# Routed attention and a PReLU feed-forward: key chunks in pairs, another first feed-forward, cluster scores on column tiles

## The chip, the cores and the metric

The kernel runs on one core of a Trainium2 chip. Its time is the device time of one execution in microseconds (us), as the median of the runs of one measurement. A profile is one further execution, taken by the hardware profiler. The engines are TensorE (PE in the rows; PEld are its weight loads), VectorE (DVE), ScalarE (ACT), GpSimd (POOL) and SyncE (SP), whose queue issues most of the DMA transfers. Each engine works through its own instructions in program order.

## The reference

Attention over 4 batches, 8 heads, 768 positions and head width 64, in which a query sees only the keys whose nearest of 16 centroids is the same; then a feed-forward of 512 to 2048 to 512 with a learned negative slope.

```
q_assign = argmax(einsum(q_n, c_n)); k_assign = argmax(einsum(k_n, c_n))
mask = q_assign[..., :, None] == k_assign[..., None, :]
scores = where(mask, q @ k.T / 8, -1e9)
attn = exp(scores - max); attn = attn / (sum(attn) + 1e-9)
x = (attn @ v) as (3072, 512)
h = x @ w_in;  g = max(h, 0) + alpha * min(h, 0);  out = g @ w_out
```

The weights of the feed-forward arrive as 64-bit floats, and the kernel makes 32-bit ones of them itself.

## The kernel before

Two heads make a pair; there are 16 pairs (4 batches of 4). The queries of a batch are worked on in two halves of 384. A **unit** (`units`, L264) is one pair, one half and one chunk of 128 keys: 6 units make a pair's half, 24 a **block** (one batch, one half), 192 the kernel. So there are 8 blocks, 0 to 7, each of which ends with one tile `xT`, the input of a feed-forward of 384 rows.

`score` (L271) multiplies a chunk of keys with the half's queries for both heads (tile `sps`, L277), takes the exponential on ScalarE (`E`, L282), zeroes on VectorE what lies in another cluster (the mask, L285), and adds `E` into `acc` on VectorE (L291, L293), from which the softmax denominators come. `weigh` (L296) multiplies `E` with the values (`vps`, L317), three units behind `score` (`LAG`). At a pair's last chunk it sums `acc` over the keys with a matmul (L306), inverts the sum (`rd`, L309), notes the lowest one (`lowest`, L312), and writes `xT` (L322). The two heads use halves of TensorE: `score` contracts over 64 rows for each head, `weigh` writes 64 columns for each; the feed-forward uses all 128 by 128. An fp32 matmul of the program shows as two rows of the profile, so `x4` at L277 or L317 is one unit.

A pair is prepared ahead of its first unit by `prep_features` (12 transposes, L208, copied by ScalarE into `qkT`, L212, with squares, L216), `prep_clusters` (12 matmuls of 32 columns, L224, and four VectorE steps up to `first`, the cluster of each position) and `prep_queries` (L251, `aq`). All of them write the one PSUM buffer of `misc()`, the tile `mps`.

The feed-forward of a block runs inside the next block, in pieces (`ffn_pieces`, L326): 16 of `hidden` (L335, then two ScalarE and one VectorE step into `gT`) and 12 of `final` (L352, into the output rows `y`). The weight conversion (`convert`, L154) takes 32 pieces: a DMA of 512 KB into `raw` (two buffers), four VectorE steps with two ScalarE steps between them, and a product on GpSimd. The conversions come from unit 20 on, two to a unit from unit 26.

The loop at L382 writes all of this out in one order for every engine: `score`, then preparation, conversions, feed-forward pieces, then `weigh`. Nothing reorders it later.

## Time and profile before

| | |
|---|---|
| median of 3 runs | 1286.82 us (1284.21 to 1287.08) |
| the profiled execution | 1280.17 us |
| its span, first to last instruction | 1278.3 us |
| busy in the span: TensorE | 1152.1 us (90%) |
| VectorE | 681.9 us (53%) |
| ScalarE | 398.9 us (31%) |
| GpSimd | 46.1 us (4%) |
| mean granted TensorE clock | 0.964 |

The span is the part that the rows below describe; the execution is 1.9 us longer. Shares are means over stages with different limits, so the rows are grouped by stage: the start up to the first exponential at 34.0 us, block 0 up to 120.7, block 1 up to 321.7, blocks 2 to 6 up to 1050.0, block 7 up to the last weighting at 1182.4, and the last feed-forward.

### The profile page before, as it was taken

How to read it: one execution, taken by the hardware profiler on the slowest of the kernel's cores; microseconds unless marked ns; L12 is line 12 of the kernel's file. 1: busy time of each engine (PE TensorE's matmuls, PEld its weight loads, DVE VectorE, ACT ScalarE, POOL GpSimd, SP SyncE). 2: the span in 40 equal slices, each digit the busy share in tenths (PEclk: the TensorE clock that was granted, in tenths of full speed). 3: DMA queues.
4: the chain of work that ended last, by engine and by line, in shares of the span. 5: the costliest groups of instructions: out<-in, count | busy, mean ns of one | idle time of the engine just before them, and what ended most of it. 6: DMA issues, size and time to landing. Idle time of an engine off the chain costs nothing.

```text
span 1278.3 us, 10850 instructions
## 1 busy us (share of the span) xinstructions
PE 1152.1 (90%) x4228; PEld 527.7 (41%) x4228; DVE 681.9 (53%) x971; ACT 398.9 (31%) x718; POOL 46.1 (4%) x57
## 2 busy tenths in 40 slices
PE   4876577689899999999899999999899999999898
PEld 3431233234444335444444334444454334433553
DVE  1689999944554464544545454644544455544210
ACT  2443354422343223322343123322343123311220
POOL 0002222300000000000000000000000000000000
PEclk9997798889999999999999999999999999999899
DMA  3302334311100010011100020011100000000000
GB/s 87 95 1 69 101 116 130 115 46 46 46 1 1 17 45 1 1 46 46 46 1 1 9 54 1 1 46 46 46 0 1 9 17 1 1 9 14 3 1 26
DMA packets 62938, 42.76 MB, mean 33 GB/s; under 512 B 51600, under 2 KB 55712, under 8 KB 62880
## 3 DMA queue, kind: packets, MB, share of 16 engines
q1 hardware_dynamic: 62592, 41.95, 11.5%
q8 instruction: 35, 0.57, 0.2%
q14 instruction: 23, 0.19, 0.0%
q10 hardware_dynamic: 288, 0.04, 0.0%
HBM read 35.69 MB, written 6.29 MB: 33 GB/s over the span
## 4 chain that ended last, share of the span: by engine, by line
PE 76%; DVE 16%; ACT 4%; issue 2%; DMA 0%; SPq 0%; ACTq 0%; DVEq 0%
PE fps L352 26%; PE fps L335 24%; PE sps L277 9%; PE vps L317 9%; DVE rd L309 4%; PE mps L224 4%; DVE E L285 3%; PE mps L208 2%; DVE gT L343 2%; DVE mant L163 1%; PE mps L251 1%; DVE mant L172 1%; ACT power L166 1%; PE mps L306 1%; DVE power L161 1%
## 5 line engine op out<-in xcount | busy, mean ns | idle before, releaser
L335 PE MATMUL fps<-xT,w_in_sb 128*128 128x384 f32 x1024 | 365.9, 512 | 36.2 <-DVE xT L322 21.1
L285 DVE SCALAR_TENSOR_TENSOR E<-aq,first,E 128x384 f32<-128x384 bf16 x384 | 226.9, 632 | 301.7 <-ACT E L282 301.3
L352 PE MATMUL fps<-w_out_sb,gT 128*128 128x512 f32 x768 | 353.7, 606 | 0.0
L282 ACT ACTIVATE E<-sps 128x768 f32<-128x768 f32 x192 | 155.7, 811 | 404.5 <-PE sps L277 291.2
L335 PEld LDWEIGHTS fps<-xT,w_in_sb 128*128 128x128 f32 x1024 | 198.9, 200 | 180.6 <-issue 50.0
L352 PEld LDWEIGHTS fps<-w_out_sb,gT 128*128 128x128 f32 x768 | 140.9, 192 | 165.4 <-issue 163.9
L343 DVE SCALAR_TENSOR_TENSOR gT<-neg,alpha_neg,gT 128x384 f32<-128x384 f32 x128 | 88.2, 693 | 179.7 <-ACT neg L342 179.1
L277 PE MATMUL sps<-qkT 64*128 64x384 f32 x768 | 182.3, 552 | 1.2 <-ACT E L282 1.1
L317 PE MATMUL vps<-E,vt 128*64 128x384 f32 x768 | 168.3, 518 | 10.1 <-DVE xT L322 9.9
L341 ACT ACTIVATE gT<-fps 128x384 f32<-128x384 f32 x128 | 62.7, 490 | 236.4 <-PE fps L335 236.4
L293 DVE TENSOR_TENSOR acc<-acc,E 128x768 f32<-128x768 f32 x128 | 122.6, 958 | 4.4
L277 PEld LDWEIGHTS sps<-qkT 64*128 64x128 f32 x768 | 59.5, 190 | 118.2 <-issue 94.1
L309 DVE RECIPROCAL rd<-mps 128x384 f32<-128x384 f32 x32 | 81.7, 2553 | 23.4 <-PE mps L306 23.4
L317 PEld LDWEIGHTS vps<-E,vt 128*64 128x64 f32 x768 | 41.8, 137 | 115.7 <-issue 85.5
L208 PE MATMUL mps<-ident,qk 128*128 128x128 f32 x192 | 35.2, 312 | 32.7 <-DVE lowest L312 29.4
L342 ACT ACTIVATE neg<-fps 128x384 f32<-128x384 f32 x128 | 62.1, 485 | 0.0
L224 PEld LDWEIGHTS mps<-cT,qkT 128*128 128x128 f32 x384 | 49.0, 209 | 10.6 <-issue 7.6
L224 PE MATMUL mps<-cT,qkT 128*128 128x32 f32 x384 | 50.8, 293 | 2.2 <-ACT qkT L212 2.2
L166 ACT ACTIVATE power<-power,low_exp 128x512 uint32<-128x512 uint32 x32 | 23.1, 722 | 80.7 <-DVE power L161 80.7
L208 PEld LDWEIGHTS mps<-ident,qk 128*128 128x128 f32 x192 | 22.7, 154 | 59.8 <-issue 50.1
L357 ACT COPY y<-fps 128x512 f32<-128x512 f32 x24 | 14.1, 586 | 94.0 <-PE fps L352 94.0
L212 ACT COPY qkT<-mps 128x512 f32<-128x512 f32 x48 | 27.9, 582 | 32.4 <-PE mps L208 32.4
(54 smaller groups left out, 389.0 us busy)
## 6 DMA issues: line engine op xcount, KB each, us to landing
raw<-in_moe_w_in_dram SPq DMA_DIRECT2D x16, 512.0 KB, 3.8
raw<-in_moe_w_out_dram SPq DMA_DIRECT2D x16, 512.0 KB, 3.5
qk<-in_q_dram SPq DMA_DIRECT2D x32, 192.0 KB, 3.5
qk<-in_k_dram SPq DMA_DIRECT2D x32, 192.0 KB, 3.5
vt<-in_v_dram SPq DMA_DIRECT2D x16, 384.0 KB, 4.2
out_dram<-y SPq DMA_DIRECT2D x24, 256.0 KB, 2.1
csb<-in_centroids_dram ACTq DMA_DIRECT2D x8, 4.0 KB, 2.5
alf<-in_moe_alpha_dram ACTq DMA_DIRECT2D x1, 8.0 KB, 2.3
```

The lines of the kernel that those rows point to most:

```text
L208: nc.tensor.transpose(out=ps[:, i * P:(i + 1) * P], in_=raw_qk[n, w][:, j].rearrange("p h d -> p (h d)"), identity=ident)
L224: nc.tensor.matmul(out=ps[:, t * W:(t + 1) * W], lhsT=qkTs[n][:, t * P:(t + 1) * P], rhs=cT[:, hp * W:(hp + 1) * W], start=True, stop=True)
L277: nc.tensor.matmul(out=ps[:, h, 0:HS], lhsT=qkT[r:r + D, S + c * P:S + (c + 1) * P], rhs=qkT[r:r + D, half * HS:(half + 1) * HS], start=Tr ...
L282: nc.scalar.activation(out=E, in_=ps[:, :, 0:HS], func=AF.Exp, scale=SCALE)
L285: nc.vector.scalar_tensor_tensor(out=E[:, h, :], in0=aqs[n, half][:, h, :], scalar=first[:, t:t + 1], in1=E[:, h, :], op0=ALU.is_equal, op ...
L293: nc.vector.tensor_tensor(out=accs[n, half], in0=accs[n, half], in1=E, op=ALU.add)
L309: nc.vector.reciprocal(out=rd, in_=ps[:, 0:HS])
L317: nc.tensor.matmul(out=po[r:r + D, 0:HS], lhsT=vts[n][:, h, c, :], rhs=E[:, h, :], start=(c == 0), stop=(c == NJ - 1))
L335: nc.tensor.matmul(out=ps[:, 0:HS], lhsT=w_in_sb[:, c, f * P:(f + 1) * P], rhs=xT[:, c, :], start=(c == 0), stop=(c == NCH - 1))
L341: nc.scalar.activation(out=gs[f], in_=ps[:, 0:HS], func=AF.Relu)
L343: nc.vector.scalar_tensor_tensor(out=gs[f], in0=neg, scalar=alpha_neg[:, f:f + 1], in1=gs[f], op0=ALU.mult, op1=ALU.add)
L352: nc.tensor.matmul(out=ps[:, 0:DM], lhsT=gs[f][:, i * P:(i + 1) * P], rhs=w_out_sb[:, f, :], start=(f == 0), stop=(f == NF - 1))
```

## The change

- **Steps.** A step is now two chunks of keys (`GROUP` = 2): 96 steps, 12 to a block, 3 to a pair's half. A step runs `score` for both chunks, then `weigh` of the step before, `mask`, `normalise` of the step before, and `add_up`; feed-forward pieces (two or three to a step), preparation and conversions follow in turn.
- **Preparation** stands at whole steps: features in a pair's third step ahead, clusters in the second, queries in the last. Up to the end of block 0, `misc()` also uses the two feed-forward PSUM buffers, which nothing else needs yet. Of pair 1 nothing is prepared ahead of the first step any more.
- **Cluster scores** are 4 matmuls of 32 output rows and 384 columns, each on its own 32 columns of TensorE (`prep_sims`), a ScalarE copy, and 3 transposes, in place of 12 matmuls of 32 columns.
- **Denominators in block 0** come from TensorE matmuls over each `E` (`sum_rows`); VectorE only adds up the sums of three steps, and `acc` is left out there.
- **Conversions** start at step 1, one to a step in block 0 and two in block 1. Each call starts one conversion and finishes the one before it. The order of the pieces is by quarters of the hidden width, and the first feed-forward takes its pieces in that order, with three partial outputs to a quarter that are added into `y` (ScalarE for the first quarter, VectorE for the others).
- **At the start**, the centroids come in one transfer instead of eight, their squares are summed on VectorE, and 40 small matmuls run on TensorE.
- The `gT` step of a hidden piece is issued with the next piece.

```diff
+    for i in range(40):
+        nc.tensor.matmul(out=warm[:, 0:P], lhsT=ident_bf, rhs=ident_bf, start=True,
+                         stop=True)
...
+        def rest():
+            nc.vector.scalar_tensor_tensor(
+                out=power, in0=hi, scalar=0x80000000, in1=power,
+                op0=ALU.bitwise_and, op1=ALU.bitwise_or)
...
+    def convert_next():
+        if sources:
+            half_converted.append(convert(*sources.popleft()))
+        if half_converted and (len(half_converted) > 1 or not sources):
+            half_converted.popleft()()
+            converted[0] += 1
...
+    def prep_sims(n):
+        hp = pairs[n][1]
+        ps = misc()
+        for g in range(NG):
+            nc.tensor.matmul(out=ps[g * W:(g + 1) * W, 0:GT * P],
+                             lhsT=cT[:, hp * W:(hp + 1) * W],
+                             rhs=qkTs[n][:, g * GT * P:(g + 1) * GT * P],
+                             start=True, stop=True)
+        simTs[n] = asg.tile([P, GT * P], FP32, name="simT")
+        nc.scalar.copy(simTs[n], ps[:, 0:GT * P])
...
+        den = None
+        if u < UB:
+            den = sum_rows(E)
+        elif s == SB - 1:
+            den = sum_rows([accs.pop((n, half))])
...
-    for u in range(NU + LAG + 1):
+    for u in range(NS + 1):
...
+        if u < NS:
             score(u)
+        if u > 0:
+            weigh(u - 1)
+        if u < NS:
+            mask(u)
+        if u > 0:
+            normalise(u - 1)
+        if u < NS:
+            add_up(u)
...
+        converting = 1 if 0 < u < UB else 2 if UB <= u < 2 * UB else 0
+        for i in range(max(take, len(prep), converting)):
+            if i < take:
+                ffn.popleft()()
+            if prep:
+                prep.popleft()()
+            if i < converting:
+                convert_next()
```

The first place is TensorE's order at the start of block 2. Before, three units there read (L317 is `weigh`, L277 `score`, L335 `hidden`, L208 and L224 the preparation; each `x2` is one chunk, both heads):

```order
L306 MATMUL mps<-acc,ones 64x384 x2
L317 MATMUL vps<-E,vt 64x384 x2
L277 MATMUL sps<-qkT 128x384 x2
L208 MATMUL mps<-ident,qk 128x128 x4
L335 MATMUL fps<-xT,w_in_sb 128x384 x8
L317 MATMUL vps<-E,vt 64x384 x2
L277 MATMUL sps<-qkT 128x384 x2
L224 MATMUL mps<-cT,qkT 128x32 x12
L335 MATMUL fps<-xT,w_in_sb 128x384 x8
L317 MATMUL vps<-E,vt 64x384 x2
L277 MATMUL sps<-qkT 128x384 x2
```

In the changed kernel a step and the start of the next read, at the same place (L388 is `weigh`, L327 `score`, L434 `hidden`, L241 the transposes, L268 and L279 the new cluster scores; each `x4` is two chunks):

```order
L327 MATMUL sps<-qkT 128x384 x4
L388 MATMUL vps<-E,vt 64x384 x4
L434 MATMUL fps<-xT,w_in_sb 128x384 x4
L268 MATMUL mps<-qkT,cT 32x384 x4
L434 MATMUL fps<-xT,w_in_sb 128x384 x4
L279 MATMUL mps<-ident,simT 128x128 x3
L327 MATMUL sps<-qkT 128x384 x4
L388 MATMUL vps<-E,vt 64x384 x4
```

Scores and weighting stand together for two chunks, the feed-forward pieces come between the pieces of preparation, and the 12 cluster matmuls have become 4 and 3 transposes with a feed-forward piece between them.

The second place is VectorE's order in block 1, where the weights are converted. Before, one unit and the mask of the next (L285 is the mask, L293 the addition to `acc`, L343 the `gT` step, L161 to L172 one conversion):

```order
L285 SCALAR_TENSOR_TENSOR E<-aq,first,E 128x384 x2
L293 TENSOR_TENSOR acc<-acc,E 128x768
L161 TENSOR_SCALAR power<-raw 128x512
L163 TENSOR_SCALAR mant<-raw 128x512
L170 SCALAR_TENSOR_TENSOR power<-raw,power 128x512
L172 SCALAR_TENSOR_TENSOR mant<-raw,mant 128x512
L161 TENSOR_SCALAR power<-raw 128x512
L163 TENSOR_SCALAR mant<-raw 128x512
L170 SCALAR_TENSOR_TENSOR power<-raw,power 128x512
L172 SCALAR_TENSOR_TENSOR mant<-raw,mant 128x512
L343 SCALAR_TENSOR_TENSOR gT<-neg,alpha_neg,gT 128x384
L285 SCALAR_TENSOR_TENSOR E<-aq,first,E 128x384 x2
```

In the changed kernel, one step there (L343 is now the mask, L361 the addition, L426 the `gT` step; L176 and L178 start a conversion, L186 and L189 finish the one before it, of other buffers):

```order
L343 SCALAR_TENSOR_TENSOR E<-aq,first,E 128x384 x4
L361 TENSOR_TENSOR acc<-acc,E 128x768 x2
L426 SCALAR_TENSOR_TENSOR gT<-neg,alpha_neg,gT 128x384 x2
L176 TENSOR_SCALAR power<-raw 128x512
L178 TENSOR_SCALAR mant<-raw 128x512
L186 SCALAR_TENSOR_TENSOR power<-raw,power 128x512
L189 SCALAR_TENSOR_TENSOR mant<-raw,mant 128x512
L176 TENSOR_SCALAR power<-raw 128x512
L178 TENSOR_SCALAR mant<-raw 128x512
L186 SCALAR_TENSOR_TENSOR power<-raw,power 128x512
L189 SCALAR_TENSOR_TENSOR mant<-raw,mant 128x512
L343 SCALAR_TENSOR_TENSOR E<-aq,first,E 128x384 x4
```

The number of instructions is that of two units with two conversions in place of four; the second start (the second L176) reads the `raw` buffer that the L186 and L189 ahead of it have just read for the last time, so its DMA is issued between them.

The third place is ScalarE's order around the first step of a pair in block 0, in the changed kernel (L335 is the exponential, L245 and L249 the copies and squares of the next pair's features, L180 and L182 the conversion):

```order
L335 ACTIVATE E<-sps 128x768 x2
L245 COPY qkT<-fps 128x512
L180 ACTIVATE power<-power,low_exp 128x512
L182 ACTIVATE mant<-mant 128x512
L245 COPY qkT<-fps 128x512
L249 ACTIVATE qk,squares<-qk 128x768
L245 COPY qkT<-mps 128x512
L249 ACTIVATE qk,squares<-qk 128x768
L335 ACTIVATE E<-sps 128x768 x2
```

The exponentials of a step now stand behind the copies, the squares and the conversion's steps of the step before.

## Rows read from the trace of the kernel before

**Rows 1.** Windows by stage: each engine's busy us (instructions), PEclk, DMA share, GB/s.
```profile
34.00:120.70 86.70, 66.28 (x330) 29.72 (x330) 71.13 (x104) 35.43 (x60) 4.44 (x3) 0.94 0.18 54
120.70:321.70 201.00, 153.76 (x515) 69.13 (x516) 156.64 (x218) 77.29 (x139) 40.05 (x29) 0.86 0.31 92
321.70:1050.00 728.30, 699.90 (x2642) 318.70 (x2641) 367.46 (x520) 222.66 (x405) 0.00 (x0) 0.99 0.08 21
1050.00:1182.40 132.40, 129.94 (x453) 54.89 (x453) 69.48 (x96) 37.03 (x64) 0.00 (x0) 1.00 0.02 7
```

**Rows 2.** Timeline of TensorE over one unit of block 4 (start us, us).
```profile
714.40 0.87 PE L317 MATMUL vps<-E,vt 128*64 128x384 f32 x4
715.19 0.92 PE L277 MATMUL sps<-qkT 64*128 64x384 f32 x4
716.04 3.70 PE L352 MATMUL fps<-w_out_sb,gT 128*128 128x512 f32 x8
719.67 0.87 PE L317 MATMUL vps<-E,vt 128*64 128x384 f32 x4
```

**Rows 3.** Timeline of TensorE where instructions of one kind stand together, at the end.
```profile
1180.38 2.16 PE L317 MATMUL vps<-E,vt 128*64 128x384 f32 x12
...
1231.51 41.36 PE L352 MATMUL fps<-w_out_sb,gT 128*128 128x512 f32 x96
```

**Rows 4.** Timeline of TensorE, the cluster scores of one pair.
```profile
562.44 2.87 PE L224 MATMUL mps<-cT,qkT 128*128 128x32 f32 x24
```

**Rows 5.** Timeline where block 3 begins: the inverse, then the feed-forward's wait.
```profile
475.57 2.55 DVE L309 RECIPROCAL rd<-mps 128x384 f32<-128x384 f32 x1
...
479.05 1.25 PE L335 MATMUL fps<-xT,w_in_sb 128*128 128x384 f32 x2 [2.46 <-DVE xT L322]
```

**Rows 6.** Timeline of VectorE in block 1 (first four) and block 4, GpSimd last.
```profile
174.20 0.41 DVE L161 TENSOR_SCALAR power<-raw 128x512 uint32<-128x512 uint32 x1
...
175.41 0.69 DVE L170 SCALAR_TENSOR_TENSOR power<-raw,power 128x512 uint32<-128x512 uint32 x1 [0.45 <-ACT power L166]
176.01 0.69 DVE L172 SCALAR_TENSOR_TENSOR mant<-raw,mant 128x512 f32<-128x512 uint32 x1
...
176.95 1.50 DVE L163 TENSOR_SCALAR mant<-raw 128x512 uint32<-128x512 uint32 x1
...
717.05 1.15 DVE L285 SCALAR_TENSOR_TENSOR E<-aq,first,E 128x384 f32<-128x384 bf16 x2 [2.18 <-ACT E L282]
718.23 0.96 DVE L293 TENSOR_TENSOR acc<-acc,E 128x768 f32<-128x768 f32 x1
...
176.78 1.39 POOL L174 TENSOR_TENSOR w_in_sb<-mant,power 128x512 f32<-128x512 f32 x1 [4.50 <-DVE mant L172]
```

**Rows 7.** ScalarE's groups by line: count, then busy us, mean ns of one.
```profile
L282 ACT ACTIVATE E<-sps 128x768 f32<-128x768 f32 x192 | 155.7, 811 | 404.5 <-PE sps L277 291.2 <-issue 99.2 <-ACT aq L254 5.9
...
L212 ACT COPY qkT<-mps 128x512 f32<-128x512 f32 x48 | 27.9, 582 | 32.4 <-PE mps L208 32.4
...
L216 ACT ACTIVATE qk<-qk 128x768 f32<-128x768 f32 x32 | 27.3, 852 | 0.0
L166 ACT ACTIVATE power<-power,low_exp 128x512 uint32<-128x512 uint32 x32 | 23.1, 722 | 80.7 <-DVE power L161 80.7
L168 ACT ACTIVATE mant<-mant 128x512 f32<-128x512 uint32 x32 | 19.9, 622 | 8.9 <-DVE mant L163 8.9
```

**Rows 8.** The tile `raw`: its DMAs from issue to landing.
```profile
DMA to landing us min/median/max: 3.4/3.8/6.0
```

**Rows 9.** Timeline of the start, and TensorE's granted clock in 40 slices of the span (page).
```profile
7.62 1.28 ACT L128 ACT_TABLE_LOAD   x1 [7.62 <-DMA alf<-in_moe_alpha_dram]
...
13.24 1.12 PE L208 MATMUL mps<-ident,qk 128*128 128x128 f32 x4 [0.27 <-DVE alpha_neg L145]
...
18.61 5.33 PE L224 MATMUL mps<-cT,qkT 128*128 128x32 f32 x24 [0.68 <-ACT qkT L212]
...
PEclk9997798889999999999999999999999999999899
```

More of the change, by code (lines that the diff above doesn't have):

```diff
@@ new lines, in score, with mask @@
+        Es[u] = []
+        for ps in pss:
+            E = epool.tile([P, 2, HS], FP32, name="E")
+            nc.scalar.activation(out=E, in_=ps[:, :, 0:HS], func=AF.Exp, scale=SCALE)
+            Es[u].append(E)
+    def mask(u):
+        n, half, s = steps[u]
+        for c, E in zip(range(s * GROUP, (s + 1) * GROUP), Es[u]):
+            for h in range(2):
+                t = slot(NJ + c, h)
+                nc.vector.scalar_tensor_tensor(
+                    out=E[:, h, :], in0=aqs[n, half][:, h, :],
+                    scalar=firsts[n][:, t:t + 1],
+                    in1=E[:, h, :], op0=ALU.is_equal, op1=ALU.mult)
@@ new lines, in add_up, with sum_rows @@
+    def add_up(u):
+        n, half, s = steps[u]
+        if u < UB:
+            return
+        E = Es[u]
+        if s == 0:
+            acc = accp.tile([P, 2, HS], FP32, name="acc")
+            nc.vector.tensor_tensor(out=acc, in0=E[0], in1=E[1], op=ALU.add)
+            accs[n, half] = acc
+            E = E[2:]
+        for e in E:
+            acc = accs[n, half]
+            nc.vector.tensor_tensor(out=acc, in0=acc, in1=e, op=ALU.add)
+    def sum_rows(srcs):
+        ps = misc()
+        for i, src in enumerate(srcs):
+            for h in range(2):
+                r = h * D
+                nc.tensor.matmul(out=ps[r:r + D, 0:HS], lhsT=ones, rhs=src[:, h, :],
+                                 start=(i == 0), stop=(i == len(srcs) - 1))
+        return ps
@@ L351, in final @@
             for f in range(f0, f0 + FQ):
                 nc.tensor.matmul(out=ps[:, 0:DM], lhsT=gs[f][:, i * P:(i + 1) * P],
-                                 rhs=w_out_sb[:, f, :], start=(f == 0),
-                                 stop=(f == NF - 1))
-            if f0 + FQ == NF:
-                y = ypool.tile([P, DM], FP32, name="y")
-                nc.scalar.copy(y, ps[:, 0:DM])
-                nc.sync.dma_start(out=rows[:, half * HJ + i, :], in_=y)
-        return ([lambda f=f: hidden(f) for f in range(NF)]
-                + [lambda i=i, f0=f0: final(i, f0)
-                   for i in range(HJ) for f0 in range(0, NF, FQ)])
+                                 rhs=w_out_sb[:, f, :], start=on and f == f0,
@@ new lines, in final @@
+                                 stop=off and f == f0 + FQ - 1)
+            if off:
+                if i not in ys:
+                    ys[i] = ypool.tile([P, DM], FP32, name="y")
+                    nc.scalar.copy(ys[i], ps[:, 0:DM])
+                else:
+                    nc.vector.tensor_tensor(out=ys[i], in0=ys[i], in1=ps[:, 0:DM],
+                                            op=ALU.add)
+                if f0 + FQ == NF:
+                    nc.sync.dma_start(out=rows[:, half * HJ + i, :], in_=ys[i])
@@ L365 @@
+        hs = [lambda f=f: hidden(f) for f in range(NF)]
+        if (b, half) == (0, 0):
+            pieces = []
+            for f0 in range(0, NF, FQ):
+                pieces += hs[f0:f0 + FQ]
+                pieces += [lambda i=i, f0=f0: final(i, f0, True, True)
+                           for i in range(HJ)]
+            return pieces
+        return hs + [lambda i=i, f0=f0: final(i, f0, f0 == 0, f0 + FQ == NF)
+                     for i in range(HJ) for f0 in range(0, NF, FQ)]
     start_of = {}
-    for u, (n, half, c) in enumerate(units):
+    for u, (n, half, s) in enumerate(steps):
@@ L377 @@
-    prep = deque(sorted(prep, key=lambda x: x[0]))
-    while prep[0][0] < 0:
-        prep.popleft()[1]()
-    load(2)
+            load_at.setdefault(max(u - 6, 0), []).append(n)
+            for g in range(len(groups)):
+                at(3, lambda n=n, g=g: prep_features(n, g))
+            at(2, lambda n=n: prep_sims(n))
+            at(2, lambda n=n: prep_clusters(n))
+        for h in range(2):
+            at(1, lambda n=n, half=half, h=h: prep_queries(n, half, h))
+    early[0] = 1
+    for piece in prep_at.pop(-1):
+        piece()
@@ new lines @@
+        if u > 0:
[6 more added lines that the diff above has]
+            add_up(u)
+        if u > 0 and u % UB == 0:
+            early[0] = 0
+            assert not ffn
+            n, half, _ = steps[u - 1]
+            ffn.extend(ffn_pieces(pairs[n][0], half))
+            whole = len(ffn)
+        if u == NS:
+            break
+        prep = deque(prep_at.get(u, []))
+        take = len(ffn) - whole * (UB - 1 - u % UB) // UB if ffn else 0
```

306 lines of the change are left out of this document (149 added, 157 removed).

## The prediction

> **What bounds the kernel now.** I read the windows by stage first, because the shares over the whole span hide that two engines take turns [rows 1]. In blocks 2 to 6 TensorE is busy for 699.9 of 728.3 us at a clock of 0.99, VectorE for half of that: TensorE is the bound, and only what shortens its own chain counts. In blocks 0 and 1 TensorE is busy for 66.3 of 86.7 and 153.8 of 201.0 us, VectorE for 71.1 and 156.6, and block 1 takes 56 us more than the mean of the later ones (728.3/5 = 145.7): there VectorE's order of work is the bound. After 1182.4 stands a bare feed-forward that the change leaves alone.
>
> Then the timeline of one unit in the TensorE-bound part [rows 2]: from one `vps` group to the next 5.27 us, made of 4 `vps` rows, 4 `sps` rows and 8 rows of the feed-forward. Where rows of one kind follow each other they cost less [rows 3]: 12 `vps` rows take 2.16 us, of which the last pair is not overlapped (a group of four takes 0.87, so eight more cost 1.29: 0.32 for two rows, which run together, one for each head); 96 feed-forward rows take 41.36, 0.43 each. The unit is then 2 x 0.64 + 8 x 0.43 = 4.73 us of streaming, and 0.54 us go to three switches: into 64-column work, into 64-row work, and back to the full array.
>
> **Blocks 2 to 7: what a step saves.** A step of two chunks has three switches where two units had six, so each of 72 steps gains 0.54 us. In three units of each block no feed-forward stood between, and a switch less was paid: I take 6.2 us a block, 37 us for six blocks. The end of the range at which nothing is saved: the 0.54 us belong to each chunk's first weight load and not to the switch. I take the full saving, because the 12 `vps` rows [rows 3] hold three chunks with three sets of weights and show no such price between them. On this the Trainium skill has a rule (TensorEngine Tiling (Array Packing), "Key Properties"): changing the tiling mode drains TensorE, changing the tile does not. By it the 37 us come whole, and the new cluster scores, a fourth mode of 32 columns between two feed-forward pieces, pay two switches more to a pair; if the rule did not hold, 0 us.
>
> **Cluster scores.** Today 24 rows for a pair [rows 4]: 2.87 us, of which the last 0.1 is overlapped, so 2.8. The new 4 matmuls are 8 rows of 384 columns. If four column tiles run together as two do, they take 2 x 0.32 = 0.64 us; two switches 0.36; three transposes 0.4 (128 columns each, a quarter of a 0.43 row, and the first one's fill): 1.4. If they don't overlap, 8 x 0.32 + 0.36 + 0.4 = 3.3. The nearest row is the two heads' `vps`, which do overlap, so I take 1.4. Of the 16 pairs 11 are prepared in blocks 2 to 6: 15 us saved, between -6 and 15. The copy between scores and transposes (0.5) lies under a feed-forward piece of 2.6 us or more.
>
> **Block ends.** `xT` now waits for `lowest`, the inverse (2.55) and four masks (2.3) on VectorE; `lowest` and `xT` itself, of 384 columns like a mask, take about 0.5 each. TensorE has the weighting (4 x 0.32) and three quarters of a hidden piece (6 x 0.32) to do meanwhile. From the denominators' end that is 0.5 + 2.55 + 2.3 + 0.5 = 5.9 less 3.2, a wait of 2.7 us, against 2.46 today [rows 5]: nothing. A shorter lag in other steps is hidden too: from its scores to its weighting a step needs 2 exponentials, 4 masks and at a pair's start the inverse, some 7.6 us, while TensorE has 10.6 us a step: 128 hidden rows of 0.32 and 96 final ones of 0.43 over 12 steps, 6.9; scores and weighting 2.6; switches, denominators and queries 1.1. If that cover went, each step would wait.
>
> Blocks 2 to 6: 728.3 - 31 - 15 = 682; block 7: 132.4 - 6 = 126; the end 95.9 as it is.
>
> **Block 1 (201 us now).** VectorE still bounds it, by a chain that the new order makes. For an ordinary step, from its first mask [rows 6]: 4 masks 2.3; 2 additions 1.9; a `gT` step 0.6; the first conversion call 1.9 (174.20 to 176.62 without its wait of 0.5 for ScalarE, which is gone). Then the second call must read a `raw` buffer whose DMA can only be issued now: 3.4 to 6.0 us, median 3.8 [rows 8]. Call two: 1.9. The next mask waits for an exponential that stands on ScalarE behind the two conversion steps of that call: 0.72 + 0.62 + 0.81 and some 0.45 until the first may start, 2.6 from the call's start, so 0.7 past its end [rows 7]. And GpSimd's product (1.39) runs just then: beside it a step of 0.42 took 1.50 [rows 6]; half of that falls into the wait, so 0.5. Sum 13.7. A pair's first step adds `lowest`, the inverse and `xT` (3.6), a third piece (0.6), takes off an addition (0.96) and the 0.7 that this covers: 16.2. Steps 0 to 9: 4 x 16.2 + 6 x 13.7 = 147; step 10 with the last conversions 12, step 11 at TensorE's pace 11, a pair's features on ScalarE in step 9 and 768 KB of loads ahead of a `raw` 2: 172 us. Bounds: with the transfer hidden (the `gT` step beside the product takes 1.7 of the 3.8 anyway) 10 x 2.1 less, 151; with landings of 6.0, 194.
>
> **Block 0 (86.7 us now).** It gets 11 conversions instead of 4, loses 20 additions of 0.96, and gains 12 small sums (0.5) on VectorE. A pair's first step: sum 0.5, `lowest` and inverse 3.0, masks 2.3, `xT` 0.5, the conversion's start; then the next exponential waits on ScalarE for the conversion (1.3), two copies (0.58) and two squares (0.85 and an accumulator read of 0.2) [rows 7]: 6.3 + 0.4 + 1.3 + 3.3 + 0.8 = 12.1. The second: sum 0.5, masks 2.3, conversion 1.9, and four cluster steps of a mask's size 2.2 = 6.9. The third is TensorE's: 12 pairs of rows x 0.32, switches and queries: 5.4. Three pairs at 24.4, less 7 for a first step without conversion and sums, and 19 for the last pair, which prepares nothing: 85; with 4 us of half clock at first, 89. Bounds 82 and 98.
>
> **The start (34.0 us now).** The centroid chain began at 7.62, after nine transfers in a row on ScalarE's queue, and the transposes at 13.24 [rows 9]. One transfer lands some 4 us earlier and one table load of 1.28 goes: -5. Three transposes with buffers of their own, instead of five rounds that wait for each copy (three of them from 13.24 to 18.61, 1.8 each): -5. Cluster scores of 5.33 become about 2.5: -3. First exponential at 21 (19 to 25). The 40 small matmuls cost nothing, as they run while TensorE waits for data; I count no gain from them.
>
> **Sum.** 21 + 89 + 172 + 682 + 126 + 96 = 1186 us of span, 92 less than 1278.3, so 1188 for the profiled execution of 1280.17. The runs' median lies 6.6 us above that execution; 1286.8 - 92 gives **1195 us**.
>
> **Rivals.**
> *The transfer in block 1 is hidden*, because VectorE is late by so much elsewhere that the data are there: 151 in place of 172, 1174 us. For it: today no VectorE step waits for `raw`. Against it: the buffer is freed by the very step ahead. 15 in 100.
> *Switches cost the same*: the 37 us stay, 1232 us. Against it stand the 12 rows of [rows 3]. 10 in 100.
> *The clock*: TensorE idles some 3 us in each step of block 1. Today the granted clock falls to 1.2 GHz in parts of that stage (slices of 0.7 and 0.8 [rows 9], mean 0.86 [rows 1]). At 0.73 TensorE's 10.6 us a step become 14.5, level with VectorE's 13.7 to 16.2, and waits on both sides add up: 20 us more, 1215. The Trainium skill (TensorE: Matmul & The Clock Gate, "Why this matters for your kernels") warns of idle gaps between bursts for the same reason. 15 in 100.
> *Slower than before*: the lag of one step does not cover its chain. Each of 72 steps would have to wait 92/72 = 1.3 us, to end at 1287 or more. It begins to wait when VectorE's work ahead of a step's last mask exceeds TensorE's 10.6 us; I count 7.6. 4 in 100.
> My forecast has 56 in 100, with 1178 to 1215 as its own range.
>
> **Numbers.** Range 1160 to 1235: below, the hidden transfer and a fast block 0; above, switches that cost the same. A measurement of this kernel tells about 0.3% from no change. Faster by more 0.95, within 0.02, slower 0.03 (the fourth rival, less what ends level).
>
> **What would show it.** Right: a mid-block step of block 4 near 10.6 us, with `sps` x8 and `vps` x8 each in about 1.4; cluster scores near 0.7; in block 1 VectorE idle about 2 us ahead of every second L176, put down to a DMA, and steps of 13 to 17 us; first exponential near 21. Wrong: `sps` x8 at 1.9, an exponential or mask that TensorE waits for in blocks 2 to 7, a clock below 0.95 there, or block 1 at TensorE's pace (130 us).

## The result, and the profile after

The changed kernel takes 1155.71 us (median of 4 runs, 1154.54 to 1159.15), the kernel before 1285.51 us on the same chip: a ratio of 0.900, 95% interval 0.8968 to 0.9032. Forecast were 1195 us and a range from 1160 to 1235. The direction was right, the gain was 39 us larger than forecast, and the time lies 4 us below the range.

Windows by stage of the changed kernel, cut at the first exponential of each block and at the last weighting; columns as in [rows 1]:

```profile
0.00:18.10 18.10, 12.39 (x80) 8.57 (x82) 3.66 (x12) 7.32 (x13) 1.78 (x26) 0.89 0.94 223
18.10:99.10 81.00, 71.07 (x386) 32.28 (x383) 68.81 (x123) 44.86 (x79) 11.45 (x9) 0.96 0.27 81
99.10:267.10 168.00, 137.32 (x465) 62.29 (x465) 118.74 (x197) 64.23 (x119) 32.58 (x23) 0.91 0.29 83
267.10:934.10 667.00, 656.04 (x2535) 313.32 (x2533) 355.35 (x524) 222.76 (x423) 0.00 (x0) 0.99 0.09 24
934.10:1061.10 127.00, 124.81 (x448) 58.04 (x444) 67.04 (x96) 35.37 (x64) 0.00 (x0) 0.99 0.02 7
1061.10:1157.30 96.20, 87.76 (x239) 44.75 (x238) 14.11 (x24) 16.31 (x36) 0.00 (x0) 0.95 0.03 12
```

| stage, us | before | forecast | after |
|---|---|---|---|
| start, to the first exponential | 34.0 | 21 | 18.1 |
| block 0 | 86.7 | 89 | 81.0 |
| block 1 | 201.0 | 172 | 168.0 |
| blocks 2 to 6 | 728.3 | 682 | 667.0 |
| block 7 | 132.4 | 126 | 127.0 |
| the last feed-forward | 95.9 | 96 | 96.2 |
| span | 1278.3 | 1186 | 1157.3 |

TensorE is still the bound of blocks 2 to 6: busy for 656.0 of 667.0 us at a clock of 0.99. More than half of the span's 28.7 us between forecast and fact lies there (15), 8 in block 0, 4 in block 1, 3 at the start.

Timeline of TensorE in block 4 of the changed kernel, which answers to [rows 2 to 4]. L327 are scores, L388 weighting, L453 final feed-forward rows, L268 and L279 the cluster scores and their transposes:

```profile
611.52 1.56 PE L327 MATMUL sps<-qkT 64*128 64x384 f32 x8
613.01 1.51 PE L388 MATMUL vps<-E,vt 128*64 128x384 f32 x8
614.45 3.70 PE L453 MATMUL fps<-w_out_sb,gT 128*128 128x512 f32 x8
618.08 0.85 PE L268 MATMUL mps<-qkT,cT 128*32 128x384 f32 x8
618.87 3.70 PE L453 MATMUL fps<-w_out_sb,gT 128*128 128x512 f32 x8
622.40 0.49 PE L279 MATMUL mps<-ident,simT 128*128 128x128 f32 x3
622.82 1.56 PE L327 MATMUL sps<-qkT 64*128 64x384 f32 x8
```

This step takes 11.3 us from scores to scores, with a pair's cluster scores in it. Eight score rows take 1.56 where twice four took 2 x 0.92 [rows 2], and the cluster scores 0.85 + 0.49 where 24 rows took 2.87 [rows 4]. Both steps show, close to the sizes forecast (1.4 and 0.7 + 0.4). What the forecast didn't have shows in the waits. TensorE's waits in blocks 2 to 6 of the kernel before (us in all, times, longest); the first row was not in the working:

```profile
PE mps L208 <- DVE lowest L312: 20.9, 10, 2.5
PE fps L335 <- DVE xT L322: 4.9, 2, 2.5
PE mps L306 <- ACT qkT L212: 2.5, 3, 0.9
```

And all of TensorE's waits in the same blocks of the changed kernel:

```profile
PE fps L434 <- DVE xT L413: 11.0, 5, 2.2
```

The ten waits of the next pair's transposes (L208, now L241) for the one `mps` buffer, which VectorE's inverse and `lowest` still read, are gone: a feed-forward piece now stands ahead of the transposes. Three of the ten stood at a block's end, as this one in block 4 of the kernel before:

```profile
624.37 0.63 PE L208 MATMUL mps<-ident,qk 128*128 128x128 f32 x4 [2.45 <-DVE lowest L312]
```

There TensorE now waits for `xT` instead, so that these waits come five times and no longer twice. To see what each kind of work costs TensorE in blocks 2 to 6, I add up the time from the start of each of its matmul rows to the start of the next, by the kind of the first; of an interval longer than 1.2 us, what exceeds 1.2 goes to the row that waited. Two experiments from below stand beside it, `e1_before_prep_late` (transposes later) and `e14_split_only` (split only):

| us in blocks 2 to 6 | before | transposes later | after | split only |
|---|---|---|---|---|
| scores | 109.5 | 102.2 | 89.4 | 101.5 |
| weighting | 94.5 | 94.5 | 85.4 | 94.5 |
| final rows | 215.6 | 214.5 | 211.1 | 211.1 |
| hidden rows, with the block-end waits | 228.4 | 221.5 | 229.5 | 222.8 |
| cluster scores | 27.0 | 26.9 | 13.2 | 13.2 |
| transposes, with their waits | 31.7 | 24.7 | 15.8 | 15.4 |
| queries and denominators | 21.6 | 24.7 | 22.5 | 22.5 |

From before to after: transposes 15.9 us less, and of the 20.1 less on scores 8.0 are the same wait (it began behind a score row, and scores with the old switches and without the wait take 101.5); switches 12.1 + 9.1 + 4.5 = 25.7 on scores, weighting and final rows; cluster scores 13.8, for ten pairs before and eleven after.

### The profile page after: what moved, and what is told of

Same layout as the page of the kernel before. It is cut to its first block, busy times and chain, and to the rows that moved or that the text cites. A ratio compares the mean times of both kernels' runs of the same rounds, so it can differ in the third digit from the quotient of the medians.

```text
span 1157.3 us, 10680 instructions
## 1 busy us (share of the span) xinstructions
PE 1089.4 (94%) x4143; PEld 519.2 (45%) x4143; DVE 627.7 (54%) x974; ACT 390.8 (34%) x731; POOL 45.8 (4%) x58
## 4 chain that ended last, share of the span: by engine, by line
PE 79%; DVE 12%; DMA 4%; ACT 3%; issue 1%; POOL 0%; DVEq 0%; ACTq 0%; POOLq 0%
PE fps L434 27%; PE fps L453 27%; PE sps L327 11%; PE vps L388 9%; DVE E L343 4%; DVE rd L405 3%; DMA raw<-in_moe_w_in_dram 2%; PE mps L368 2%; DMA raw<-in_moe_w_out_dram 2%; PE mps L241 1%; DVE mant L189 1%; DVE power L186 1%; DVE power L176 1%; PE mps L268 1%; PE mps L304 1%
## 5 line engine op out<-in xcount | busy, mean ns | idle before, releaser
L434 PE MATMUL fps<-xT,w_in_sb 128*128 128x384 f32 x1024 | 364.0, 506 | 21.4 <-DVE xT L413 17.6
L453 PE MATMUL fps<-w_out_sb,gT 128*128 128x512 f32 x768 | 353.1, 608 | 20.3 <-POOL w_out_sb L192 7.6
L343 DVE SCALAR_TENSOR_TENSOR E<-aq,first,E 128x384 f32<-128x384 bf16 x384 | 212.5, 615 | 180.1 <-ACT E L335 180.0
L434 PEld LDWEIGHTS fps<-xT,w_in_sb 128*128 128x128 f32 x1024 | 192.2, 195 | 176.1 <-issue 39.4
L453 PEld LDWEIGHTS fps<-w_out_sb,gT 128*128 128x128 f32 x768 | 142.2, 192 | 200.9 <-issue 188.4
L335 ACT ACTIVATE E<-sps 128x768 f32<-128x768 f32 x192 | 145.5, 812 | 107.1 <-PE sps L327 72.6
L327 PE MATMUL sps<-qkT 64*128 64x384 f32 x768 | 155.4, 524 | 1.7 <-ACT E L335 1.7
L388 PE MATMUL vps<-E,vt 128*64 128x384 f32 x768 | 144.8, 494 | 0.0
L426 DVE SCALAR_TENSOR_TENSOR gT<-neg,alpha_neg,gT 128x384 f32<-128x384 f32 x128 | 76.9, 615 | 84.8 <-ACT neg L442 84.2
L361 DVE TENSOR_TENSOR acc<-acc,E 128x768 f32<-128x768 f32 x112 | 106.9, 954 | 1.9
L327 PEld LDWEIGHTS sps<-qkT 64*128 64x128 f32 x768 | 68.1, 192 | 61.0 <-issue 29.8
L388 PEld LDWEIGHTS vps<-E,vt 128*64 128x64 f32 x768 | 52.0, 136 | 78.0 <-issue 65.1
L403 DVE TENSOR_REDUCE lowest<-mps 128x1 f32<-128x384 f32 x28 | 15.6, 556 | 124.2 <-PE mps L368 124.2
L405 DVE RECIPROCAL rd<-mps 128x384 f32<-128x384 f32 x28 | 71.3, 2547 | 0.0
L180 ACT ACTIVATE power<-power,low_exp 128x512 uint32<-128x512 uint32 x32 | 23.1, 723 | 96.3 <-DVE power L176 96.3
L307 ACT CAST aq<-mps 128x384 bf16<-128x384 f32 x57 | 27.5, 482 | 52.6 <-PE mps L304 52.5
L245 ACT COPY qkT<-mps 128x512 f32<-128x512 f32 x40 | 23.6, 590 | 24.1 <-PE mps L241 24.1
L176 DVE TENSOR_SCALAR power<-raw 128x512 uint32<-128x512 uint32 x32 | 13.5, 422 | 32.1 <-DMA raw<-in_moe_w_out_dram 18.1
L304 PEld LDWEIGHTS <-first 128*128 128x128 bf16 x192 | 15.5, 99 | 31.0 <-issue 22.9
```

Of the source, the lines that this page charges most:

```text
L307: nc.scalar.copy(aqs[n, half][:, h, :], ps[:, 0:HS])
L327: nc.tensor.matmul(out=ps[:, h, 0:HS], lhsT=qkT[r:r + D, S + c * P:S + (c + 1) * P], rhs=qkT[r:r + D, half * HS:(half + 1) * HS], start=Tr ...
L335: nc.scalar.activation(out=E, in_=ps[:, :, 0:HS], func=AF.Exp, scale=SCALE)
L343: nc.vector.scalar_tensor_tensor(out=E[:, h, :], in0=aqs[n, half][:, h, :], scalar=firsts[n][:, t:t + 1], in1=E[:, h, :], op0=ALU.is_equal ...
L361: nc.vector.tensor_tensor(out=acc, in0=acc, in1=e, op=ALU.add)
L388: nc.tensor.matmul(out=po[r:r + D, 0:HS], lhsT=vts[n][:, h, c, :], rhs=e[:, h, :], start=(c == 0), stop=(c == NJ - 1))
```

## Experiments

Medians, ratios to the kernel before on the same chip, and the stages of the profiled execution. Stages that an edit doesn't touch differ by up to 3 us between profiles, and the kernel before took 1280.91 to 1285.51 us beside these runs, so a difference of a few us between two totals says little. Code is abridged: `...` and remarks in brackets stand for lines that are not shown.

| kernel | us | ratio, 95% interval | start | block 0 | block 1 | blocks 2 to 6 |
|---|---|---|---|---|---|---|
| after | 1155.71 | 0.900 [0.8968, 0.9032] | 18.1 | 81.0 | 168.0 | 667.0 |
| e1_before_prep_late | 1261.72 | 0.9824 [0.9784, 0.9864] | 34.3 | 91.5 | 197.8 | 709.1 |
| e2_split_steps | 1246.06 | 0.9714 [0.9676, 0.9752] | 16.9 | 86.0 | 181.9 | 727.9 |
| e14_split_only | 1185.74 | 0.9243 [0.9195, 0.929] | 17.8 | 86.1 | 173.2 | 681.0 |
| e3_old_clusters | 1175.76 | 0.9162 [0.9125, 0.9198] | 16.8 | 84.4 | 168.4 | 683.8 |
| e4_raw3 | 1131.64 | 0.8816 [0.8781, 0.8851] | 18.1 | 79.6 | 146.9 | 665.4 |
| e7_whole_conv | 1139.96 | 0.8898 [0.8872, 0.8923] | 17.8 | 83.1 | 151.3 | 663.7 |
| e8_old_ffn_order | 1175.13 | 0.9167 [0.9142, 0.9192] | 17.4 | 80.2 | 188.4 | 667.0 |
| e6_dve_den | 1161.72 | 0.9066 [0.9038, 0.9093] | 17.9 | 90.7 | 165.9 | 665.4 |
| e12_one_buffer | 1171.58 | 0.9132 [0.9085, 0.9179] | 21.5 | 94.4 | 167.9 | 665.4 |
| e11_eight_loads | 1155.73 | 0.9023 [0.8966, 0.908] | 20.5 | 78.6 | 167.1 | 667.0 |
| e5_no_warm | 1150.99 | 0.8973 [0.8947, 0.8998] | 17.0 | 80.3 | 168.2 | 667.1 |
| e13_together | 1112.27 | 0.8667 [0.8622, 0.8711] | 18.2 | 79.7 | 142.1 | 652.8 |

**The missed wait, alone in the kernel before.**

```
         score(u)
-        if prep and prep[0][0] <= u + 5: ...
...      (conversions, feed-forward pieces)
+        if prep and prep[0][0] <= u + 5: ...
         weigh(w)
```

> The kernel before, with one thing altered: in each unit the piece of preparation stands behind the feed-forward piece, just ahead of the weighting, and no longer straight behind the scores. Nothing else of the change is in it. Theory (a wait that the prediction left out): in the trace of before TensorE waits 20.9 us in 10 waits in 321.7 to 1050 us at the transposes of the next pair, for the one buffer that VectorE's inverse and minimum of the denominators still read, and 29.4 us in the whole span; with a feed-forward piece of some 3.4 us ahead of them these waits are gone, the time falls by 10 to 25 us (1260 to 1276), and blocks 2 to 6 by 10 to 16 us from 728.3. Rival: the buffer is as scarce as before, so the wait only moves to the denominators or the queries, and the time stays within 4 us of before.

Measured: 1261.72 us against 1280.91 for the kernel before, 19 us less, and blocks 2 to 6 at 709.1 from 728.3, also 19 less, a little more than expected. All waits of TensorE in blocks 2 to 6 that this kernel's trace lists:

```profile
PE mps L306 <- ACT qkT L212: 8.3, 10, 1.0
PE fps L335 <- DVE xT L322: 7.0, 5, 2.5
```

The 20.9 us at L208 are gone; 5.8 came back at the denominators (L306), which now stand behind the transposes' copies, and 2.1 at `xT`. The rival saw that much rightly, but not that the rest stays gained. Moving one call by one feed-forward piece is worth 1.8%. By the table of kinds 14.3 of the 19 come off scores and transposes, 6.9 off hidden rows, 1.1 off final rows, and 3.1 go to queries and denominators. The hidden rows are cheaper because fewer of them run at 1.2 GHz. In the kernel before the granted clock falls to 0.50 six times in blocks 2 to 6, each time at a wait of 2.3 to 2.5 us, and hidden rows then take 0.64 us from start to start instead of 0.32: 26 such rows cost 8.3 us more than at the upper level. In this run it falls once, and 2 such rows cost 0.6. A window of the kernel before, behind its wait at 769.77 us (columns as in [rows 1]):

```profile
770.00:773.00 3.00, 3.00 (x5) 1.62 (x6) 2.35 (x4) 0.87 (x2) 0.00 (x0) 0.50 0.00 0
```

**The switches.** First with a feed-forward piece between the two chunks:

```
-        score(u); weigh(u - 1); mask(u)
+        for part in range(2):
+            score(u, part); weigh(u - 1, part); mask(u, part)
+            if part == 0 and ffn and u % UB:
+                ffn.popleft()()
```

> The changed kernel with the two chunks of a step apart again: scores, weighting and mask of the first chunk, one feed-forward piece, then those of the second; all else stays. Theory (the price is of the switch between kinds): three switches come back in each of 72 steps of blocks 2 to 7 and 12 of block 1, at 0.54 us for three, so 39 to 45 us more than the changed kernel (1195 to 1201), some 32 us of them in blocks 2 to 6. Rival (the price is of the first weight load of each chunk, whatever stands ahead): nothing more in blocks 2 to 6, and under 5 us in all. Third (it also keeps ScalarE and VectorE fed in smaller lumps, so that block 0 gets shorter): block 0 falls below 78 us from 81.0.

Measured: 90 us more than the changed kernel, 61 of them in blocks 2 to 6, twice what the theory gives. TensorE's waits in blocks 2 to 6 of this kernel say why:

```profile
PE mps L304 <- ACT aq L307: 18.9, 20, 1.2
PE fps L439 <- DVE xT L418: 8.9, 5, 1.8
PE mps L279 <- ACT simT L273: 6.6, 11, 0.6
PE mps L241 <- ACT qkT L245: 6.5, 8, 1.0
```

The edit also used up a feed-forward piece that had stood between two pieces of preparation, so that the second waited for ScalarE's copy of the first: 32 us of waits that the changed kernel doesn't have. The third theory falls: block 0 is 5 us longer. The run mixed two prices, so the split was repeated without the piece in between (the two lines with `ffn` left out).

> The changed kernel with the two chunks of a step apart, scores and weighting of the first and then of the second, and no feed-forward piece between them; pieces and preparation stay where the change has them. Per step two switches come back (weighting to scores, scores to weighting), 120 in blocks 2 to 6. Theory (the price is of the switch): 0.14 to 0.2 us each, so blocks 2 to 6 take 17 to 24 us longer (684 to 691), and the 36 us beyond that in the run with a feed-forward piece between were waits of the preparation for ScalarE's copies. Rival (the price is of a chunk's first weight load): 0 to 3 us longer. Second rival (that run's surplus is of the split itself): 50 us or more longer.

Measured: 30 us more than the changed kernel; blocks 2 to 6 at 681.0, 14 us longer, below the theory's 17 to 24. Timeline of a step in block 4:

```profile
604.77 0.92 PE L327 MATMUL sps<-qkT 64*128 64x384 f32 x4
605.61 0.87 PE L393 MATMUL vps<-E,vt 128*64 128x384 f32 x4
606.41 0.92 PE L327 MATMUL sps<-qkT 64*128 64x384 f32 x4
607.25 0.87 PE L393 MATMUL vps<-E,vt 128*64 128x384 f32 x4
```

Scores are back at the 0.92 of [rows 2]. By the table of kinds, scores and weighting cost 12.1 + 9.1 = 21.2 us more for 120 switches, 0.18 each, a third of the 0.54 that the forecast had for three. The net is smaller because the hidden rows with the block-end waits take 6.7 less; the listed waits for `xT` fall from 11.0 to 8.9 us, and 13 hidden rows that run at 1.2 GHz in the changed kernel (4.2 us more than at the upper level) have no counterpart here. They stand behind three of its five waits for `xT`, as in this window:

```profile
410.00:413.00 3.00, 3.00 (x6) 1.57 (x5) 0.62 (x1) 0.33 (x1) 0.00 (x0) 0.50 0.00 0
```

Both rivals fall: the price is neither zero nor 50 us. Of the 47 us by which blocks 2 to 6 of the first split are longer still, 38 stand on rows of preparation and denominators (32 of them the waits above), and 9 on hidden and final rows, for the third switch.

**Cluster scores.**

```
-        for g in range(NG): matmul(ps[g * W:(g + 1) * W, ...], lhsT=cT, rhs=qkT)
-        simT = copy(ps); 3 transposes
+        for t in range(NB): matmul(ps[:, t * W:(t + 1) * W], lhsT=qkT, rhs=cT)
```

> The changed kernel with the cluster scores as before: 12 matmuls of 32 columns with the tokens as weights in place of four column tiles, the copy and three transposes. Theory: 2.7 us of TensorE for a pair against 1.3 (27.0 and 13.2 us in the ten pairs of blocks 2 to 6), so 14 us more in blocks 2 to 6 and 16 to 19 us more in all. Rival: a part of the 12 matmuls' time hides in waits of TensorE that the copy of the column tiles makes; then under 8 us in all.

Measured: 16.8 us more in blocks 2 to 6 and 20 in the total, a little above the theory. Both kernels prepare eleven pairs there, not ten: 28.6 us of cluster scores against 13.2. The column tiles pay in full; TensorE doesn't wait for the copy between them.

**Block 1: the transfer of the raw weights.** Three buffers instead of two:

```
-    raws = tile_pool(name="raws", bufs=2)
+    raws = tile_pool(name="raws", bufs=3)
-    accp = tile_pool(name="accp", bufs=2)
+    accp = tile_pool(name="accp", bufs=1)
```

> The changed kernel with three buffers for the raw weights in place of two (and one accumulator of the denominators in place of two, to make room; the accumulator is read by TensorE before its next writer comes). Theory: VectorE's waits for the raw transfers (32 us in 12 long waits in block 1, the longest 4.0) are what makes the steps of block 1 longer than the 8.8 to 10.4 us of the later ones; then block 1 falls by 15 to 30 us from 168.0, and the time to 1125 to 1141. Rival: VectorE and ScalarE are themselves full there (conversions, masks, sums), so that the wait moves to the next engine, and block 1 falls by under 8 us.

Measured: block 1 at 146.9, 21 us less, and 1131.64 us. VectorE's longest waits in block 1, the changed kernel first, then with three buffers:

```profile
DVE power L176 <- DMA raw<-in_moe_w_out_dram: 18.1, 6, 3.7
DVE power L176 <- DMA raw<-in_moe_w_in_dram: 12.8, 4, 4.0
DVE y L461 <- PE fps L453: 11.8, 5, 5.0
DVE E L343 <- ACT E L335: 5.7, 8, 2.0
```

```profile
DVE y L461 <- PE fps L453: 9.2, 4, 4.7
DVE E L343 <- ACT E L335: 7.3, 7, 2.5
DVE power L176 <- POOL w_out_sb L192: 5.8, 5, 1.4
DVE power L176 <- POOL w_in_sb L192: 3.9, 4, 1.2
```

Of 30.9 us of waits for transfers none is left; 9.7 came back as waits for GpSimd's products, which hold the converted halves. The other way to free the buffer early is to finish a conversion in the call that starts it:

```
-            half_converted.append(convert(*sources.popleft()))
-        if half_converted and (len(half_converted) > 1 or not sources):
-            half_converted.popleft()()
+            convert(*sources.popleft())()
```

> The changed kernel with each conversion done whole in one call, where the change does its second half one call later. Theory (the late second half holds the raw buffer, and so delays the next transfer): VectorE's 30.8 us of waits for transfers in block 1 mostly go, and waits of 0.5 us for ScalarE come back in some 21 conversions (10 us), so block 1 falls by 8 to 20 us from 168.0. Rival (splitting pays by itself, because VectorE no longer waits for ScalarE, and transfers would be late in any case): block 1 rises by 5 us or more.

Measured: block 1 at 151.3, 17 us less, as the theory has it. Finishing late, which the change added, costs more than it saves while there are two raw buffers: VectorE's waits for ScalarE are back, and are cheap.

```profile
DVE power L186 <- ACT power L180: 9.4, 19, 1.0
```

**Block 1: the order of the first feed-forward.**

```
-        if (b, half) == (0, 0):   (hidden and final pieces by quarters)
+        if False:
```

and the conversions in that order, all of `w_in` first.

> The changed kernel with the first feed-forward in the old order: all 16 hidden pieces, then the 12 final ones, and the weights converted in that order too. Theory (VectorE's chain sets the steps of block 1, and the order of TensorE's pieces is of no matter): block 1 within 5 us of 168.0, with 9 additions of rows to the output less on VectorE. Rival (the order by converted weights is what keeps TensorE from waiting for GpSimd's products): 8 us or more longer. Third (the order makes its own waits: 20 us of TensorE's waits in block 1 stand ahead of final rows): 8 us or more shorter.

Measured: block 1 at 188.4, 20 us longer. The theory falls and the first rival holds: the order matters. TensorE's longest wait in that block is now

```profile
PE fps L453 <- POOL w_out_sb L192: 28.1, 7, 6.0
```

In the old order the first output rows need all 32 conversions at once: by the exponentials, steps 7 and 8 take 29.7 and 23.9 us, where the changed kernel has 13.7 and 13.5. The forecast had priced block 1 in the new order and so contained this without a term of its own.

**Block 0.**

```
-        if u < UB:
-            return             (in add_up: E now goes into acc on VectorE in block 0 too)
...
-        if u < UB:
-            den = sum_rows(E)
-        elif s == SB - 1:
+        if s == SB - 1:
             den = sum_rows([accs.pop((n, half))])
```

> The changed kernel with the denominators of block 0 added up by VectorE again, and summed by TensorE once for a pair, as in the other blocks. Theory (VectorE's chain bounds block 0, busy 68.8 of 81.0 us): it gets 20 additions of 0.96 more and some 10 sums of 0.55 less, so block 0 takes 11 to 14 us longer (92 to 95), and the total as much. Rival (what bounds block 0 is ScalarE's order and TensorE's own work; VectorE is waited for only in part): under 6 us.

Measured: block 0 at 90.7, 9.7 us longer, somewhat under the theory; VectorE is busy for 80.8 us in it (68.8 after). Blocks 1 to 6 are 4 us shorter in that profile and the rest 3, so its span is only 2.7 us longer; the medians differ by 6. VectorE sets the pace of block 0, but the sums are not all in its way.

```
-    early[0] = 1
```

> The changed kernel with the small results of the start and of block 0 on one PSUM buffer, where the change lets two of three use the feed-forward's buffers, which are free there. The prediction gave these buffers 5 us of the start and nothing in block 0. Theory: first exponential 3 to 6 us later (21 to 24), and block 0 longer by 5 to 12 us (86 to 93), because transposes, queries and the twelve sums of denominators then wait for each other's readers; 8 to 18 us in all. Rival (the copies lie beside other work): under 4 us in all.

Measured: first exponential at 21.5 (+3.4), block 0 at 94.4 (+13.4), 16 us in the total: the theory's range, block 0 a little above it. TensorE's longest waits from the start to the end of block 0 are now those of the transposes for ScalarE's copy out of the one buffer:

```profile
PE mps L241 <- ACT qkT L245: 14.6, 8, 5.2
```

The borrowed buffers are worth more in block 0, where the forecast counted nothing for them, than at the start. Part of the 3.4 us at the start can be the clock: the granted clock is 0.58 in 8 to 14 us of this run, where the changed kernel has 1.00.

**The start.**

```
-    nc.scalar.dma_start(out=cen, in_=centroids.rearrange("h c d -> (h c) d"))
+    for h in range(H):
+        nc.scalar.dma_start(out=cen[h * NC:(h + 1) * NC, :], in_=centroids[h])
```

> The changed kernel with the centroids fetched by eight transfers on ScalarE's queue in place of one; all else stays. The prediction gave the one transfer and the one table load 5 us of the start together. Theory: the eight transfers come back as 3 to 5 us, so the first exponential at 21 to 23 us instead of 18.1. Rival (the first exponential waits for the transfers of the first pair's data and the transposes, and the centroids are there in time either way): under 1 us.

Measured: first exponential at 20.5, 2.4 later, under the theory's 3 to 5 but more than the rival's 1; yet block 0 ends at 99.1 in both, and the totals are equal. Windows of the two kernels (columns as in [rows 1]), the changed one first:

```profile
14.00:17.00 3.00, 1.59 (x10) 1.10 (x12) 1.28 (x3) 1.04 (x3) 0.00 (x0) 0.50 1.12 264
17.00:21.00 4.00, 4.00 (x18) 2.62 (x15) 2.04 (x4) 3.32 (x5) 0.00 (x0) 0.53 0.66 259
```

```profile
14.00:17.00 3.00, 1.14 (x7) 0.31 (x3) 1.17 (x3) 1.01 (x3) 0.00 (x0) 1.00 0.76 166
17.00:21.00 4.00, 3.06 (x24) 2.15 (x25) 0.85 (x2) 2.65 (x4) 0.00 (x0) 1.00 1.02 311
```

And the scores of step 0, in the changed kernel and with eight transfers:

```profile
16.16 2.93 PE L327 MATMUL sps<-qkT 64*128 64x384 f32 x8
```

```profile
18.38 1.56 PE L328 MATMUL sps<-qkT 64*128 64x384 f32 x8
```

TensorE gets its data earlier in the changed kernel, but at 1.2 GHz: the eight rows take 2.93 instead of 1.56, the transposes behind them are slower too, and the lead is gone at step 1, whose scores start at 21.32 and 21.36. With eight transfers the stretch at 1.2 GHz came earlier (granted clock 0.72 in 8 to 14 us, 1.00 in the changed kernel).

```
-    for i in range(40):
+    for i in range(1):
```

> The changed kernel with one small matmul in place of the 40 that run while TensorE waits for the first data. The prediction's theory: they bring nothing, the first exponential stays at 18 us and the total within 4 us of the changed kernel. Rival (they lift the clock: in the changed kernel the granted clock is at its upper level from 20.8 us on, before the change only from 49.4 us): block 0 grows from 81.0 to 85 or more, because TensorE works at 1.2 GHz for its first 20 to 30 us, and the first exponential comes 1 to 2 us later; 4 to 10 us in all.

Measured: 1150.99 us, block 0 at 80.3, first exponential at 17.0. The rival falls, and the small matmuls gain nothing, as forecast; the 4.7 us between the medians lie within the scatter (1149.05 to 1157.48 here, 1154.54 to 1159.15 with them). But that they cost nothing, because TensorE waits for data meanwhile, doesn't hold. Timeline of the changed kernel, then of this one:

```profile
1.73 4.45 PE L130 MATMUL vps<-ident_bf 128*128 128x128 bf16 x40 [1.73 <-POOL ident_bf L117]
6.11 0.69 PE L153 MATMUL mps<-ident,cn 128*64 128x128 f32 x2
8.09 0.66 PE L241 MATMUL fps<-ident,qk 128*128 128x128 f32 x4
```

```profile
4.04 0.69 PE L153 MATMUL mps<-ident,cn 128*64 128x128 f32 x2 [2.03 <-DVE cn L144]
6.34 1.11 PE L241 MATMUL fps<-ident,qk 128*128 128x128 f32 x4
```

The centroids' matmul (L153) has its data by 4.06 us in both, but in the changed kernel it stands behind the 40 until 6.11. The transposes (L241) then start 1.75 us later and run faster, 0.66 us for four instead of 1.11; the first exponential is still 1.1 us later.

**What is still to be had.** Three buffers for raw and for converted weights, and at a block's end

```
+        if u > 0 and (u % UB == 0 or u == NS):
+            normalise(u - 1)
         if u < NS:
             mask(u)
-        if u > 0:
+        if u > 0 and not (u % UB == 0 or u == NS):
             normalise(u - 1)
```

> The changed kernel with three things: three buffers for raw weights, three for converted halves (others cut to make room), and at a block's end the normalised rows ahead of the masks on VectorE. Theories: the block-end wait is VectorE's masks, so 17 us in 7 waits become about 4, and blocks 2 to 6 fall by 8 to 11 us from 665 to 667; in block 1 VectorE's waits of 9.7 us for GpSimd's product, which the run with three raw buffers alone still had, go, and block 1 falls to 137 to 143 us from its 146.9. Total 1108 to 1118. Rivals: the masks that are now later delay the next weighting by as much, and blocks 2 to 6 stay within 3 us; in block 1 TensorE is the bound at 132 us busy, and nothing more is to be had (over 145).

Measured: 1112.27 us, 0.8667 of the kernel before (0.8622 to 0.8711), where the changed kernel has 0.900. Blocks 2 to 6 fall by 12.6 to 14.2 us, more than expected, and block 1 to 142.1; both rivals fall. The hidden rows at 1.2 GHz are gone in blocks 2 to 6, and TensorE's waits for `xT` are down from 11.0 us to

```profile
PE fps L434 <- DVE xT L413: 1.5, 4, 0.4
```

## Why the prediction was wrong

**The step that failed** is the sum "Blocks 2 to 6: 728.3 - 31 - 15 = 682". It holds the two terms that the edit names, switches and cluster scores, and lets all else stay. But the change also puts a feed-forward piece between the denominators and the next transposes, and with it the 20.9 us of waits at L208 go, which the trace of the kernel before lists. The working read waits only at block ends [rows 5]. The run with the transposes later shows 19 us for this alone; in the table of kinds it is 24 between before and after (15.9 + 8.0). Less 5 and 1 for the two sizes below and 2 that queries and hidden rows cost more, this is the 15 us by which the sum was off.

The 15 us are the largest part of the miss, not the only one. The time lies 4 us below the range, so it would have come to lie inside if any one of three parts had been as forecast: these 15, the 8 of block 0, or the 10 of the base.

**Two sizes in the same sum.** Switches: 31 forecast, 25.7 in the table. For two of a step's three switches the price of 0.18 each is confirmed, as 120 more of them cost 21.2 us; the third, between these and the full array, gave 4.5 us on final rows where 31 - 21.2 = 9.8 had been counted (what it gave on hidden rows, the waits there cover). The rule of the Trainium skill (TensorEngine Tiling (Array Packing), "Key Properties"), that a change of mode drains TensorE and a change of tile does not, agrees with both: the changes of mode cost this, and eight rows on four column tiles take 0.85 us, no more than four rows of scores. Cluster scores: 15 forecast, 13.8 in the table; by pairs 2.7 us became 1.2, a saving of 1.5 where 1.4 was forecast, but the kernel before prepares only ten pairs in blocks 2 to 6.

**Block ends: "nothing".** The single wait came out at 2.2 us, where 2.7 were worked out and 2.46 read. But the waits for `xT` in blocks 2 to 6 rose from 4.9 us to 11.0: [rows 5] is one of only two before, because at the other three block ends TensorE stood at the transposes (7.3 of the 20.9 us). So all the listed waits together went from 28.3 us to 11.0, 17.3 less, and the rows at 1.2 GHz behind them gave 4.1 more (8.3 to 4.2). That the block-end wait can go almost altogether by another order on VectorE was not asked.

**Block 1: 172, measured 168.** Each mechanism is shown: VectorE's waits for raw transfers (30.9 us, up to 4.0 each), ordinary steps of 13.1 to 13.7 for 13.7, first steps of 14.8 to 15.0 for 16.2; the last pair's first two steps, 16.0 and 16.2, stand against 18.2 and 12, so step 10 was forecast too short. That removing the wait gives 21 us (151 was the bound with the transfer hidden; 146.9 measured) makes the first rival the next change, not this one.

**Block 0: 89, measured 81.** The two middle pairs take 22.2 us each instead of 24.4 (10.5, 4.6 and 7.1 for 12.1, 6.9 and 5.4: the first ScalarE copy starts before the inverse ends, and the four cluster steps fall into the third step), and the 4 us added for half clock did not appear: the granted clock was 0.96. The kernel before had more to lose there than [rows 1] say: the record of its clock begins only at 49.4 us, and up to then its rows run at 1.2 GHz, four rows of scores in 1.65 us instead of 0.92:

```profile
45.98 1.65 PE L277 MATMUL sps<-qkT 64*128 64x384 f32 x4
49.48 0.92 PE L277 MATMUL sps<-qkT 64*128 64x384 f32 x4
```

How much of the 5.7 us between before and after in this block is the clock, no run separates.

**The start: 21, measured 18.1,** but its parts were misjudged. The single transfer gives 2.4 us that are lost again by step 1; the borrowed buffers give up to 3.4 at the start and 13 in block 0; the 40 small matmuls, counted as free, delay the first exponential by 1.1.

**The base.** 1286.8 - 92 took the median's distance from the profiled execution (6.6 us above it) as lasting. After the change the median lies 3.4 below its profiled execution (1159.15). That is 10 of the 39 us, and no matter of the kernel.

Of the rivals, equal switches and the clock in block 1 (0.91, above the 0.86 of before) did not come; the lag of one step is covered: no wait for an exponential or a mask stands among TensorE's in blocks 2 to 6.

## What to carry to other kernels

When a change moves code, list every wait of the bounding engine whose waiter or releaser moves, not only the waits the edit is about: here the largest unnoticed gain was one shared PSUM buffer read by a slow inverse, and one piece of other work ahead of its next user hid it. Small work that goes through another engine's copy needs such a piece between each two; a run that uses the pieces up elsewhere (as the first split) pays twice. And forecast a difference between profiled executions, and widen it by how far a single execution stands from the median.

## What the runs showed of the hardware

- A first exponential 2.4 us earlier was worth nothing: TensorE's granted clock was 0.50 and 0.53 in 14 to 17 and 17 to 21 us, 1.00 in both in the kernel with eight transfers, and 0.81 and 0.72 in the one without the 40 small matmuls. All three have a stretch at 1.2 GHz ahead of 21 us; what differs is the work that it falls on, the transposes with eight transfers (1.11 us for four instead of 0.66) and the scores of step 0 in the changed kernel (2.93 for 1.56). What moves it the runs don't show.
- A wait can cost more than its length: at six waits of 2.3 to 2.5 us in blocks 2 to 6 of the kernel before the granted clock fell to 0.50, and the hidden rows behind them took 0.64 us instead of 0.32, 8.3 us in all. It didn't fall at two others of 2.45.
- The record of the granted clock can begin late: at 49.4 us in the trace before, with rows at 1.2 GHz ahead of that in windows that the profile gives as 1.00. Durations of equal rows tell the level there.
- A change between scores on 64 rows and weighting on 64 columns costs about 0.18 us (21.2 us for 120).
- Eight rows on four column tiles of 32 take 0.85 us, as long as four rows of scores or weighting do (0.92 and 0.87).
- Two preparation pieces in a row cost TensorE up to 1.2 us each time for a ScalarE copy of 0.48; 20 such waits came to 18.9 us.
